# VectorE joins a weight's words in the PSUM bank; other low halves by VectorE; turns moved

## The chip, the cores and the metric

The kernel runs on one core of one Trainium2 chip. The metric is device time in microseconds (us) of one execution, as the median of several runs; less is better. In this program TensorE (PE) multiplies matrices into PSUM, of which eight banks are used; ScalarE (ACT) and VectorE (DVE) work elementwise on PSUM and on SBUF, the main on-chip memory; GpSimd (POOL) works elementwise on SBUF; SyncE (SP) issues the transfers from and to DRAM.

## What is computed

The reference chains three stages over 4 sequences of 768 positions. All arrays are float32; the kernel is handed the three big weights' float64 bits (a low and a high 32-bit word for each number).

```python
for t in range(S):                                   # gated linear attention, 8 heads of 48
    state = alpha[:, :, t, :, None] * state + einsum('bhd,bhe->bhde', k[:, :, t], v[:, :, t])
    y[:, :, t] = einsum('bhd,bhde->bhe', q[:, :, t], state)
x = y as (B, S, 384)
h = maximum(x @ w_in, 0)                             # moe: w_in 384 x 1024
conv_out = three taps of conv_w along S over h       # zero at both ends
x = (h * sigmoid(conv_out)) @ w_out                  # w_out 1024 x 384
xn = layernorm(x) * g_ln                             # moe2
out = x + maximum(xn @ w_ch1, 0) @ w_ch2             # w_ch1 384 x 1536, w_ch2 1536 x 384
```

## The kernel before

The positions are cut into 12 blocks of 256. A block passes through attention (two chunks of 128 positions each, 24 chunks in all), the first feed-forward part (`moe1_*`, 8 slices j of 128 hidden columns), a norm, and the second one (`moe2_a`, 12 slices). Every large product is done in split precision: an operand is a "high" fp32r part and a "low" fp32r rest, and high x high, high x low and low x high are added in PSUM: nine TensorE products for a slice going in (L604 for moe1, L803 for moe2) and six for a slice going out (L690).

**Weights.** w1 (w_in) and w2 (w_out) come in 4 pieces of 2 slices each, w3 (w_ch1) and w4 (w_ch2) in 6. `convert_weight` turns a piece (128 x 768 numbers) into its high and low part. ScalarE copies the scaled high word (L257, to z) and the top byte (L261). VectorE joins both with the rest of the exponent (L264), then puts the sign in (L267): z is now the weight in float32. ScalarE rounds z to the high part (L306). The low part is z minus high, made in one of two ways that the table `LOWS` picks for w1 to w4: "pe" (TensorE multiplies z with an identity matrix and adds minus the high part, L310 and L311, one PSUM bank of 384 columns at a time; ScalarE copies the bank out, L314), or "pool" (one GpSimd subtraction, L317). `LOWS` is pe, pe, pool, pe; the second halves of w3 and w4 follow `LOW2`, pool. An identity product counts as two TensorE entries in the trace.

**Slices.** For moe1, ScalarE clips the slice and makes the first tap (L612, L616), VectorE adds two taps (L620), ScalarE takes the sigmoid (L635), VectorE multiplies (L638), ScalarE copies the high part (L652), and the low part is a VectorE subtraction (L660), or, for the first `BY_PE` blocks, a TensorE product (L354) and a ScalarE copy (L658). Three PSUM banks hold slices ("h"), three hold sums ("acc"), two serve attention and the weights ("att"). An attention chunk costs VectorE two scans (L408, L424) and two maskings (L459), GpSimd two products (L420, L428), and TensorE scores (L450), a transposition (L474), outputs (L518) and a state update (L534).

**Order.** Everything is a step with a turn, a number from the constants at the top (`FIRST`, `LEAD`, `SPACING` and `FETCH` for chunks, `LOADS` and `CONVERT` with their paces for weights, `LAG` from a slice going in to the same slice going out). `Plan.order` places steps one by one on the five engines: of the steps that are ready on an engine, the one with the lowest turn goes first, with costs that it estimates. The result is a fixed order for each engine; on the chip, an engine works its queue strictly in that order and waits on semaphores.

Of the kernel before, what the change touches and what calls it, by code (L numbers as in the profile page):

```python
# [9 lines left out]
F32R = mybir.dt.float32r  # L10
# [11 lines left out]
DM = H * D  # L22
# [22 lines left out]
XN = 1   # L45
X1 = 2 
WAIT = 6
LAG = 5
FIRST = -16, -15, -14, -4, 2
LEAD = 4  # L50
SPACING = 2
FETCH = 12
LOADS = -17, -16, -4, -9.5
LOAD_PACE = 1
CONVERT = -17, -9, 8, 10
CONVERT_PACE = 1.25, 1, 1 
BY_PE = 2, 0
LATER = 0, 8
LOW2 = "pool" 
LOWS = "pe", "pe", "pool", "pe"   # L60


class Plan:
# [137 lines left out]
def act_us(n, scaled=False):  # L201
    return 0.165 + 0.00083 * n + 0.093 * scaled


def dve_us(n, rate=1):
    return 0.15 + 0.00104 * rate * n


def pool_us(n):
    return 0.13 + 0.00215 * n  # L210
# [7 lines left out]
def attn_moe_kernel(ctx: ExitStack, tc, qka, vv, qka_t, v_t, w_in, conv_w, w_out, g_ln, w_ch1, w_ch2, out):  # L218
# [32 lines left out]
    def from_f64(z, raw, n):  # L251

        low, high = raw[:, :n, 0], raw[:, :n, 1]
        zi = z.bitcast(I32)

        def first():
            act.activation(out=z, in_=high.bitcast(F32), func=ACTF.Copy, scale=2.0 ** -112)  # L257

        def top():
            byte = raw[:, :n, :].bitcast(U8)[:, :, 3]  # L260
            act.activation(out=low, in_=byte, func=ACTF.Copy, scale=1 / 32, bias=-15.5 / 32)  # L261

        def join():
            dve.scalar_tensor_tensor(  # L264
                out=zi, in0=zi, scalar=3, in1=low, op0=ALU.logical_shift_left, op1=ALU.bitwise_or
            )
            dve.scalar_tensor_tensor(  # L267
                out=zi, in0=high, scalar=-(2 ** 31), in1=zi, op0=ALU.bitwise_and, op1=ALU.bitwise_or
            )

        yield first
        yield top
        yield join

    raw_w = {}

    def weight_tile(n, j, dtype):
        return const.tile([128, PIECE, 2, DM], dtype, tag=f"w{n}_{j}", name=f"w{n}_{j}", bufs=1)
# [12 lines left out]
    def convert_weight(n, dst, j):  # L291
# [6 lines left out]
            t["f"] = list(from_f64(t["z"], raw.rearrange("p (n w) -> p n w", w=2), m))  # L298
            t["f"][0]()

        def high():
            t["w"] = weight_tile(n, j, F32R)
            for i in range(PIECE):
                dst[j * PIECE + i] = t["w"][:, i]
            t["z"] = t["z"].rearrange("p (j f) -> p j f", j=PIECE)
            act.activation(out=t["w"][:, :, 0], in_=t["z"], func=ACTF.Copy)  # L306

        def low_products(i):
            t[i] = bank("att", "low")[:, :DM]
            pe.matmul(out=t[i], lhsT=ident, rhs=t["z"][:, i], start=True, stop=False)  # L310
            pe.matmul(out=t[i], lhsT=minus, rhs=t["w"][:, i, 0], start=False, stop=True)  # L311

        def low_half(i):
            act.activation(out=t["w"][:, i, 1], in_=t[i], func=ACTF.Copy)  # L314
# [3 lines left out]

        add("act", act_us(m), first, r=[w], new=[z])
        add("act", act_us(m), lambda: t["f"][1](), w=[w])  # L320
        add("dve", 2 * dve_us(m), lambda: t["f"][2](), r=[w], w=[z], port=True)
        add("act", act_us(m), high, r=[z], w=[w])
        low = LOW2 if n > 2 and j >= F2 // 2 // PIECE else LOWS[n - 1]
        if low == "pe":
            for i in range(PIECE):
                b = ring("att", 2)
                add("pe", 0.9, lambda i=i: low_products(i), r=[z, w], new=[b], mode="full")
                add("act", act_us(DM), lambda i=i: low_half(i), r=[b], w=[w])
        elif low == "dve":
            add("dve", dve_us(m), lambda: rest(dve), r=[z], w=[w], port=True)  # L330
        else:
            add("pool", pool_us(m), lambda: rest(pool), r=[z], w=[w], port=True)


    def causal(t):
# [600 lines left out]
    def load_small():  # L936
# [7 lines left out]
        add("sp", dma_us(220), load, new=[("cwr", 0)])  # L944
        add("act", act_us(24), lambda: t["f"][0](), r=[("cwr", 0)], w=[("cw", 0)])
        add("act", act_us(24), lambda: t["f"][1](), w=[("cwr", 0)])
        add("dve", 0.36, lambda: t["f"][2](), r=[("cwr", 0)], w=[("cw", 0)])


    tasks = []  # L950
# [220 lines left out]
```

## Time and profile before

| what | us |
|---|---|
| median of 3 runs (684.97, 686.26, 686.45) | 686.26 |
| the profiled execution, own time | 685.02 |
| its span, first to last instruction | 683.2 |
| first VectorE instruction on a weight (L264) | at 14.15 |
| first moe1 product (L604) | at 53.86 |
| first tap of a moe1 slice on VectorE (L620) | at 57.37 |
| first moe2 product (L803) | at 119.29 |
| last group of products (L690) | at 674.03 |

The profile lists each instruction with start and duration in us from the span's start. An own time is 1.82 us more than its span. TensorE's clock has two levels, 1.2 and 2.4 GHz; the profile gives the mean granted clock of a stretch as a share of the higher one.

### The profile page before, as it was taken

What the parts mean: (1) busy time and instruction counts of PE and PEld (TensorE: products, weight loads), DVE (VectorE), ACT (ScalarE), POOL (GpSimd) and SP (SyncE); (2) the same over time, 40 slices, a digit from 0 to 9 for tenths busy, and PEclk for the clock granted to TensorE, in tenths of its full rate; (3) what the DMA queues carried; (4) which work ended last, traced back from release to release, by engine and by line L of the source; (5) the groups of instructions that cost most, each with busy time, mean ns of one, the idle gap of its engine ahead of it and who ended that gap; (6) DMA issues with size and microseconds to landing.
All of it is one profiled execution on the core that took longest, in us unless ns stands there. A gap on an engine that the chain in (4) does not pass through costs nothing.

```text
span 683.2 us, 14211 instructions
## 1 busy us (share of the span) xinstructions
PE 649.7 (95%) x5788; PEld 612.6 (90%) x5788; DVE 432.5 (63%) x865; ACT 328.6 (48%) x795; POOL 123.9 (18%) x190
## 2 busy tenths in 40 slices
PE   3887999999999999999999999999999999999995
PEld 2546887989999999999999999999999999999994
DVE  5586999898468379448468379358468457365221
ACT  3678799755245236345345346345245335254210
POOL 4052342461121031101021031101021000000000
PEclk9979999999999999999999999999999999999998
DMA  9997201112112012102012012102001000000000
GB/s 316 319 393 229 71 2 48 52 57 64 57 58 76 5 57 81 57 1 80 1 58 79 2 58 80 57 1 81 1 16 39 1 2 24 1 24 1 2 24 27
DMA packets 15736, 44.50 MB, mean 65 GB/s; under 512 B 1472, under 2 KB 4672, under 8 KB 15664
## 3 DMA queue, kind: packets, MB, share of 16 engines
q1 hardware_dynamic: 15664, 43.52, 19.5%
q8 instruction: 47, 0.77, 0.5%
q14 instruction: 25, 0.20, 0.1%
HBM read 38.80 MB, written 4.72 MB: 64 GB/s over the span
## 4 chain that ended last, share of the span: by engine, by line
PE 89%; DVE 4%; ACT 3%; DMA 1%; issue 1%; POOL 0%; SPq 0%; ACTq 0%
PE acc L690 37%; PE h L803 23%; PE h L604 15%; PE y L518 5%; PE s L450 4%; PE u L534 2%; PE low L310 1%; PE h L759 1%; DMA raw<-in_qka 1%; PE kt L474 1%; DVE z L267 1%; DVE z L264 1%; ACT w L261 1%; ACT z L257 0%; ACT w L314 0%
## 5 line engine op out<-in xcount | busy, mean ns | idle before, releaser
L690 PE MATMUL acc<-w,gh 128*128 128x384 f32 x960 | 250.9, 342 | 0.0
L690 PEld LDWEIGHTS acc<-w,gh 128*128 128x128 f32 x960 | 160.9, 188 | 3.4 <-issue 0.8
L690 PE MATMUL acc<-w,gl 128*128 128x384 f32 x480 | 161.3, 336 | 0.0
L816 DVE SCALAR_TENSOR_TENSOR gl<-h,gh 128x256 fp32r<-128x256 f32 x144 | 60.4, 422 | 153.8 <-ACT gh L811 151.9
L811 ACT ACTIVATE gh<-h 128x256 fp32r<-128x256 f32 x144 | 55.3, 384 | 186.5 <-PE acc L690 168.3
L803 PE MATMUL h<-xnh,w 128*128 128x256 f32 x864 | 127.5, 283 | 0.0
L803 PEld LDWEIGHTS h<-xnh,w 128*128 128x128 f32 x864 | 118.4, 188 | 1.0 <-DVE a L424 0.4
L620 DVE SCALAR_TENSOR_TENSOR cv<-h,cw,cv 128x256 f32<-128x256 f32 x192 | 92.2, 481 | 28.5 <-ACT cv L616 24.0
L604 PE MATMUL h<-xh,w 128*128 128x258 f32 x576 | 87.4, 288 | 4.4 <-ACT gl L658 3.3
L690 PEld LDWEIGHTS acc<-w,gl 128*128 128x128 f32 x480 | 90.1, 188 | 0.0
L604 PEld LDWEIGHTS h<-xh,w 128*128 128x128 f32 x576 | 79.5, 191 | 7.7 <-ACT gl L658 4.5
L803 PE MATMUL h<-xnl,w 128*128 128x256 f32 x432 | 74.9, 282 | 0.0
L612 ACT ACTIVATE h<-h 128x258 f32<-128x258 f32 x96 | 35.7, 372 | 61.7 <-PE h L604 59.2
L803 PEld LDWEIGHTS h<-xnl,w 128*128 128x128 f32 x432 | 61.6, 188 | 0.0
L604 PE MATMUL h<-xl,w 128*128 128x258 f32 x288 | 50.4, 283 | 0.0
L635 ACT ACTIVATE cv<-cv 128x256 f32<-128x256 f32 x96 | 39.7, 415 | 21.1 <-DVE cv L620 20.8
L616 ACT ACTIVATE cv<-h,cw 128x256 f32<-128x256 f32 x96 | 45.3, 473 | 1.6
L638 DVE TENSOR_TENSOR h<-h,cv 128x256 f32<-128x256 f32 x96 | 40.6, 424 | 8.2 <-ACT cv L635 5.5
L411 POOL COPY ends<-later 112x4 f32<-112x4 f32 x24 | 5.9, 245 | 217.6 <-DVE later L408 217.6
L428 POOL TENSOR_TENSOR a<-raw,a 112x512 f32<-112x512 f32 x24 | 30.1, 1254 | 69.7 <-DVE a L424 68.4
L604 PEld LDWEIGHTS h<-xl,w 128*128 128x128 f32 x288 | 41.6, 191 | 0.2 <-POOL xl L580 0.2
L652 ACT ACTIVATE gh<-h 128x256 fp32r<-128x256 f32 x96 | 35.8, 380 | 10.2 <-DVE h L638 8.6
(90 smaller groups left out, 778.6 us busy)
## 6 DMA issues: line engine op xcount, KB each, us to landing
raw<-in_qka SPq DMA_DIRECT2D x23, 673.8 KB, 4.7
w<-in_moe_w_ch SPq DMA_DIRECT2D x12, 768.0 KB, 15.3
vraw<-in_vv SPq DMA_DIRECT2D x24, 256.0 KB, 2.7
out<-x SPq DMA_DIRECT2D x11, 384.0 KB, 2.8
w<-in_moe_w_in SPq DMA_DIRECT2D x4, 768.0 KB, 13.3
w<-in_moe_w_out SPq DMA_DIRECT2D x4, 768.0 KB, 14.4
raw<-in_qka SPq DMA_DIRECT2D x1, 448.0 KB, 3.8
out<-x SPq DMA_DIRECT2D x2, 192.0 KB, 3.8
```

Of the source, the lines that this page charges most:

```text
L518: pe.matmul(out=ps[32 * n:32 * n + 32, k * C:(k + 1) * C], lhsT=l, rhs=r, start=m < 4, stop=m >= len(products) - 4, skip_group_check=True,)
L604: pe.matmul(out=ps[:, :T + 2], lhsT=w1[j][:, l, k * 128:(k + 1) * 128], rhs=r[:, k, :], start=n == 0, stop=n == 3 * K1 - 1,)
L612: act.activation(out=t["h"], in_=t["h"], func=ACTF.Relu)
L616: act.activation(out=t["cv"], in_=t["h"][:, 0:T], func=ACTF.Copy, scale=cw[:, 0, j:j + 1])
L620: dve.scalar_tensor_tensor(out=t["cv"], in0=t["h"][:, k:k + T], scalar=cw[:, k, j:j + 1], in1=t["cv"], op0=ALU.mult, op1=ALU.add,)
L635: act.activation(out=t["cv"], in_=t["cv"], func=ACTF.Sigmoid)
L638: dve.tensor_tensor(out=t["h"][:, :T], in0=t["h"][:, 1:T + 1], in1=t["cv"], op=ALU.mult)
L652: act.activation(out=m_t[0, i, j][0], in_=t["h"][:, :T], func=ACTF.Copy)
L690: pe.matmul(out=acc_t[s, i][t][:, :DM], lhsT=l[:, ts], rhs=w[j][:, r], start=j in firsts and n == 0, stop=j + 1 in lasts and n == 2,)
L803: pe.matmul(out=ps[:, :T], lhsT=w3[j][:, l, k * 128:(k + 1) * 128], rhs=r[:, k, :], start=n == 0, stop=n == 3 * K1 - 1,)
L811: act.activation(out=m_t[1, i, j][0], in_=u["ps"][:, :T], func=ACTF.Relu)
L816: dve.scalar_tensor_tensor(out=lo, in0=u["ps"][:, :T], scalar=0.0, in1=hi, op0=ALU.max, op1=ALU.subtract)
```

## The change

Four things change. (1) A "pe" weight gets its low part without the identity: TensorE first writes any product into the bank (`opens`), VectorE writes the joined words with the sign straight into that bank (`sign`, L269 of the new file), ScalarE copies the high part out of the bank, TensorE adds minus the high part to it (`less`), and ScalarE copies the low part out. (2) `LOWS` becomes pe, dve, dve, dve: only w1 goes that way; w2 and the first halves of w3 and w4 get their low part by one VectorE subtraction (L335 of the new file) with both inputs in SBUF. (3) `BY_PE` goes from 2 to 1 block, so block 1's eight low parts move from TensorE and ScalarE to VectorE. (4) The turns move.

```diff
-LAG = 5
-FIRST = -16, -15, -14, -4, 2
+LAG = 4
+FIRST = -12, -15, -14, -6, 2
...
-BY_PE = 2, 0
+BY_PE = 1, 0
...
-LOWS = "pe", "pe", "pool", "pe" 
+LOWS = "pe", "dve", "dve", "dve" 
...
+        def sign(to=z, part=slice(0, n)):
             dve.scalar_tensor_tensor(
-                out=zi, in0=high, scalar=-(2 ** 31), in1=zi, op0=ALU.bitwise_and, op1=ALU.bitwise_or
+                out=to.bitcast(I32), in0=high[:, part], scalar=-(2 ** 31), in1=zi[:, part],
+                op0=ALU.bitwise_and, op1=ALU.bitwise_or,
             )
...
+        banks = [ring("att", 2) for _ in range(PIECE)] if low == "pe" else []
+
+        def opens(i):
+
             t[i] = bank("att", "low")[:, :DM]
-            pe.matmul(out=t[i], lhsT=ident, rhs=t["z"][:, i], start=True, stop=False)
-            pe.matmul(out=t[i], lhsT=minus, rhs=t["w"][:, i, 0], start=False, stop=True)
+            pe.matmul(
+                out=t[i].rearrange("p (k c) -> p k c", k=K1), lhsT=minus,
+                rhs=minus.rearrange("p (o c) -> p o c", o=1).to_broadcast([128, K1, 128]), start=True, stop=True,
+            )
+
+        def sign(i):
+
+            t["f"][3](t[i], slice(i * DM, (i + 1) * DM))
+
+        def high(i=None):
+            if "w" not in t:
+                t["w"] = weight_tile(n, j, F32R)
+                for m in range(PIECE):
+                    dst[j * PIECE + m] = t["w"][:, m]
+            if i is None:
+                t["z"] = t["z"].rearrange("p (j f) -> p j f", j=PIECE)
+                act.activation(out=t["w"][:, :, 0], in_=t["z"], func=ACTF.Copy)
+            else:
+                act.activation(out=t["w"][:, i, 0], in_=t[i], func=ACTF.Copy)
...
+        if not banks:
+            add("dve", 2 * dve_us(m), lambda: (t["f"][2](), t["f"][3]()), r=[w], w=[z], port=True)
+            add("act", act_us(m), high, r=[z], w=[w])
+            engine, us = (dve, dve_us(m)) if low == "dve" else (pool, pool_us(m))
+            add(low, us, lambda: rest(engine), r=[z], w=[w], port=True)
+            return
+        add("dve", dve_us(m), lambda: t["f"][2](), r=[w], w=[z], port=True)
+        for i, b in enumerate(banks):
+            add("pe", 0.000458 * DM, lambda i=i: opens(i), new=[b], mode="full")
+            add("dve", dve_us(DM), lambda i=i: sign(i), r=[w, z], w=[b])
+        for i, b in enumerate(banks):
+            add("act", act_us(DM), lambda i=i: high(i), r=[b], w=[w])
+            add("pe", 0.000458 * DM, lambda i=i: less(t[i], t["w"][:, i, 0]), r=[w], w=[b], mode="full")
+            add("act", act_us(DM), lambda i=i: low_half(i), r=[b], w=[w])
```

The other constants: `LEAD` 4 to 8, `SPACING` 2 to 3, `FETCH` 12 to 10, `LOADS` third value -4 to -8, `CONVERT` from -17, -9, 8, 10 to -19, -9, 9, 11, its paces from 1.25, 1, 1 to 1.25, 1.25, 1.5, `LATER` from 0, 8 to 2, 8. In the new file a line below the changed functions stands 20 lines further down.

What the constants decide is the order of each queue. The first place is VectorE's queue from its first weight piece on. In the rows, z is the joined weight, w1_0 the raw piece 0 of w1, low a PSUM bank, s the scores and pm the masked ones, u and y the update and the outputs of attention. Before:

```order
L264 SCALAR_TENSOR_TENSOR z_158<-z_158,w1_0_109 128x768
L267 SCALAR_TENSOR_TENSOR z_158<-w1_0_109,z_158 128x768
L543 COPY state_80<-u_187 48x4x48 x2
L571 TENSOR_TENSOR xl_203<-y_165,xh_198 128x3x128
L264 SCALAR_TENSOR_TENSOR z_196<-z_196,w2_0_111 128x768
L267 SCALAR_TENSOR_TENSOR z_196<-w2_0_111,z_196 128x768
L459 TENSOR_TENSOR pm_232<-s_210,mask_63 128x512
L459 TENSOR_TENSOR pm_232<-s_211,mask_63 128x512
```

Now:

```order
L264 SCALAR_TENSOR_TENSOR z_144<-z_144,w1_0_113 128x768
L269 SCALAR_TENSOR_TENSOR low_100<-w1_0_113,z_144 128x384
L269 SCALAR_TENSOR_TENSOR low_109<-w1_0_113,z_144 128x384
L479 TENSOR_TENSOR pm_173<-s_150,mask_63 128x512
L264 SCALAR_TENSOR_TENSOR z_163<-z_163,w2_0_115 128x768
L269 SCALAR_TENSOR_TENSOR z_163<-w2_0_115,z_163 128x768
L479 TENSOR_TENSOR pm_173<-s_151,mask_63 128x512
L264 SCALAR_TENSOR_TENSOR z_182<-z_182,w1_1_117 128x768
L269 SCALAR_TENSOR_TENSOR low_186<-w1_1_117,z_182 128x384
L335 TENSOR_TENSOR w2_0_212<-z_163,w2_0_212 128x2x384
L563 COPY state_80<-u_216 48x4x48 x2
```

The sign of a w1 piece is written in two halves into PSUM banks, a w2 piece gets a third VectorE instruction (L335), and chunk 0's maskings now come behind the first weight piece. From VectorE's first weight instruction to the last one ahead of the first tap the queue held 37 instructions and holds 53.

The second place is TensorE's queue around the first moe1 product (h from xh and xl, the two parts of block 0). Before:

```order
L310 MATMUL low_484<-z_374,ident_61 128x384
L311 MATMUL low_484<-w1_3_414,minus_62 128x384
L604 MATMUL h_495<-xh_198,w1_0_206 128x258 x6
L604 MATMUL h_495<-xl_203,w1_0_206 128x258 x3
L604 MATMUL h_508<-xh_198,w1_0_206 128x258 x6
L604 MATMUL h_508<-xl_203,w1_0_206 128x258 x3
L604 MATMUL h_520<-xh_198,w1_1_302 128x258 x6
L604 MATMUL h_520<-xl_203,w1_1_302 128x258 x3
L310 MATMUL low_536<-z_456,ident_61 128x384
L311 MATMUL low_536<-w2_3_518,minus_62 128x384
```

Now:

```order
L470 MATMUL s_493<-a_462,later_393 128x128
L624 MATMUL h_503<-xh_227,w1_0_175 128x258 x6
L624 MATMUL h_503<-xl_240,w1_0_175 128x258 x3
L624 MATMUL h_520<-xh_227,w1_0_175 128x258 x6
L624 MATMUL h_520<-xl_240,w1_0_175 128x258 x3
L494 MATMUL kt_535<-ident_61,later_393 128x112 x4
L624 MATMUL h_541<-xh_227,w1_1_242 128x258 x6
L624 MATMUL h_541<-xl_240,w1_1_242 128x258 x3
L538 MATMUL y_560<-a_462,state_80 32x128 x12
L538 MATMUL y_560<-pm_516,vraw_351 32x128 x16
```

No identity products stand here any more, and the scores of chunk 3, which followed behind the first three slices, now stand ahead of them.

The third place is VectorE's queue at the end of the two moe1 blocks, up to the second xnl, the low part of the normed block 0, which the first moe2 slice needs. Before:

```order
L264 SCALAR_TENSOR_TENSOR z_1122<-z_1122,w3_3_469 128x768
L267 SCALAR_TENSOR_TENSOR z_1122<-w3_3_469,z_1122 128x768
L638 TENSOR_TENSOR h_1103<-h_1103,cv_1141 128x256
L620 SCALAR_TENSOR_TENSOR cv_1199<-h_1143,cw_64,cv_1199 128x256 x2
L778 TENSOR_TENSOR xnl_1209<-h_1179,xnh_1201 128x3x128
L638 TENSOR_TENSOR h_1143<-h_1143,cv_1199 128x256
L459 TENSOR_TENSOR pm_1229<-s_1211,mask_63 128x512
L459 TENSOR_TENSOR pm_1229<-s_1212,mask_63 128x512
L408 SCALAR_TENSOR_TENSOR later_1276<-raw_1192,from_one_78 112x516
L778 TENSOR_TENSOR xnl_1209<-h_1225,xnh_1201 128x3x128
```

Now:

```order
L269 SCALAR_TENSOR_TENSOR z_945<-w3_3_391,z_945 128x768
L658 TENSOR_TENSOR h_1075<-h_1075,cv_1101 128x256
L640 SCALAR_TENSOR_TENSOR cv_1151<-h_1110,cw_64,cv_1151 128x256 x2
L680 TENSOR_TENSOR gl_1167<-h_1075,gh_1164 128x256
L798 TENSOR_TENSOR xnl_1170<-h_1123,xnh_1139 128x3x128
L658 TENSOR_TENSOR h_1110<-h_1110,cv_1151 128x256
L479 TENSOR_TENSOR pm_1184<-s_1141,mask_63 128x512
L680 TENSOR_TENSOR gl_1190<-h_1110,gh_1186 128x256
L798 TENSOR_TENSOR xnl_1170<-h_1172,xnh_1139 128x3x128
```

The subtractions of block 1 (L680) are new on this queue, and a scan of attention (L408) has left it. From the first tap to this second xnl the queue held 92 instructions and holds 95.

## Rows read from the trace of the kernel before

**Rows 1.** The page: busy us and share of the span by engine.
```profile
PE 649.7 (95%) x5788; PEld 612.6 (90%) x5788; DVE 432.5 (63%) x865; ACT 328.6 (48%) x795; POOL 123.9 (18%) x190
```
**Rows 2.** Busy time by stretch, with granted clock, DMA share and GB/s last.
```profile
14.15:57.37 43.22, 35.81 (x299) 23.81 (x300) 30.81 (x38) 30.78 (x55) 13.18 (x16) 0.88 1.03 352
57.37:119.29 61.92, 55.56 (x519) 48.85 (x517) 54.57 (x93) 54.80 (x125) 20.18 (x24) 0.97 0.21 65
80.00:100.00 20.00, 18.79 (x179) 16.80 (x178) 19.28 (x33) 16.84 (x42) 8.35 (x12) 1.00 0.09 31
119.29:674.20 554.91, 554.22 (x4951) 537.14 (x4951) 338.80 (x725) 238.83 (x611) 84.02 (x128) 1.00 0.12 37
674.20:683.20 9.00, 0.51 (x3) 0.19 (x2) 1.08 (x2) 0.00 (x0) 0.00 (x0) 0.66 0.15 50
```
**Rows 3.** VectorE's waits, 12 to 57.4 us: on whom, total, times, longest.
```profile
DVE z L264 <- ACT w L261: 7.2, 3, 4.7
DVE cv L620 <- ACT cv L616: 2.8, 1, 2.8
DVE state L545 <- PE u L534: 1.4, 1, 1.4
```
**Rows 4.** VectorE's waits, 57.4 to 119.29 us.
```profile
DVE h L638 <- ACT cv L635: 3.3, 2, 1.9
DVE pm L459 <- PE s L450: 1.0, 1, 1.0
```
**Rows 5.** TensorE's instructions in order of time: start, us, line, operation.
```profile
53.86 0.99 PE L604 MATMUL h<-xh,w 128*128 128x258 f32 x6 [1.06 <-POOL xh L580]
...
85.40 0.28 PE L354 MATMUL h<-gh,minus 128*128 128x256 f32 x1
85.52 0.89 PE L604 MATMUL h<-xh,w 128*128 128x258 f32 x6
...
86.61 0.81 PE L310 MATMUL low<-z,ident 128*128 128x384 f32 x2
...
87.43 0.89 PE L604 MATMUL h<-xh,w 128*128 128x258 f32 x6
...
119.29 0.88 PE L803 MATMUL h<-xnh,w 128*128 128x256 f32 x6
...
674.03 0.51 PE L690 MATMUL acc<-w,gh 128*128 128x384 f32 x2
```
**Rows 6.** The chain that ended last: one chunk's outputs on TensorE.
```profile
116.54 1.67 PE y L518 x56
```
**Rows 7.** VectorE's instructions in order of time, and GpSimd's beside the slow one.
```profile
14.15 1.57 DVE L264 SCALAR_TENSOR_TENSOR z<-z,w 128x768 int32<-128x768 int32 x1
...
33.05 0.96 DVE L267 SCALAR_TENSOR_TENSOR z<-w,z 128x768 int32<-128x768 int32 x1
33.93 1.23 DVE L408 TENSOR_TENSOR_SCAN later<-raw,from_one 112x516 f32<-112x516 f32 x1
...
36.01 1.17 POOL L420 TENSOR_TENSOR later<-raw,later 112x512 f32<-112x512 f32 x1
36.04 1.96 DVE L267 SCALAR_TENSOR_TENSOR z<-w,z 128x768 int32<-128x768 int32 x1
...
47.57 0.68 DVE L459 TENSOR_TENSOR pm<-s,mask 128x512 f32<-128x512 f32 x1
...
48.38 1.29 DVE L424 TENSOR_TENSOR_SCAN a<-raw,from_end 112x516 f32<-112x516 f32 x1
```
**Rows 8.** Groups of instructions: count, busy us, mean ns, idle before.
```profile
L660 DVE TENSOR_TENSOR gl<-h,gh 128x256 fp32r<-128x256 f32 x80 | 32.7, 418 | 6.8 <-ACT gh L652 4.6 <-PE h L604 0.5
L571 DVE TENSOR_TENSOR xl<-y,xh 128x384 fp32r<-128x384 f32 x24 | 13.1, 546 | 1.9 <-ACT xh L565 1.9
L314 ACT ACTIVATE w<-low 128x384 fp32r<-128x384 f32 x22 | 10.7, 488 | 6.2 <-PE low L311 6.0
L658 ACT ACTIVATE gl<-h 128x256 fp32r<-128x256 f32 x16 | 6.1, 381 | 1.0 <-PE h L354 0.3
```

More of the change, by code (lines that the diff above doesn't have):

```diff
@@ L47 @@
 WAIT = 6
-LAG = 5
-FIRST = -16, -15, -14, -4, 2
[L50 to L53, printed above, removed]
+LAG = 4
+FIRST = -12, -15, -14, -6, 2
+LEAD = 8
+SPACING = 3
+FETCH = 10
+LOADS = -17, -16, -8, -9.5
 LOAD_PACE = 1
-CONVERT = -17, -9, 8, 10
-CONVERT_PACE = 1.25, 1, 1
-BY_PE = 2, 0
-LATER = 0, 8
+CONVERT = -19, -9, 9, 11
+CONVERT_PACE = 1.25, 1.25, 1.5
+BY_PE = 1, 0
+LATER = 2, 8
 LOW2 = "pool"
-LOWS = "pe", "pe", "pool", "pe"
+LOWS = "pe", "dve", "dve", "dve"
 class Plan:
@@ L273, in from_f64 @@
         yield join
+        yield sign
     raw_w = {}
@@ L299, in first @@
             t["f"][0]()
[L301 to L308, printed above, removed]
-            t[i] = bank("att", "low")[:, :DM]
-            pe.matmul(out=t[i], lhsT=ident, rhs=t["z"][:, i], start=True, stop=False)
-            pe.matmul(out=t[i], lhsT=minus, rhs=t["w"][:, i, 0], start=False, stop=True)
+        low = LOW2 if n > 2 and j >= F2 // 2 // PIECE else LOWS[n - 1]
+        banks = [ring("att", 2) for _ in range(PIECE)] if low == "pe" else []
+        def opens(i):
+            t[i] = bank("att", "low")[:, :DM]
+            pe.matmul(
[14 more added lines that the diff above has]
+                act.activation(out=t["w"][:, i, 0], in_=t[i], func=ACTF.Copy)
         def low_half(i):
@@ L320, in convert_weight @@
         add("act", act_us(m), lambda: t["f"][1](), w=[w])
[L321 to L332, printed above, removed]
+        if not banks:
[12 more added lines that the diff above has]
+            add("act", act_us(DM), lambda i=i: low_half(i), r=[b], w=[w])
     def causal(t):
@@ L946, in load_small @@
         add("act", act_us(24), lambda: t["f"][1](), w=[("cwr", 0)])
-        add("dve", 0.36, lambda: t["f"][2](), r=[("cwr", 0)], w=[("cw", 0)])
+        add("dve", 0.36, lambda: (t["f"][2](), t["f"][3]()), r=[("cwr", 0)], w=[("cw", 0)])
     tasks = []
```

## The prediction

> **What bounds the kernel now.** I read the page's engine shares first: TensorE is busy for 95% of the span [rows 1], which seems to say that the change, which takes products away from it, is a gain. A share over the whole span hides stages, so next I cut the span where the work changes: at VectorE's first weight instruction, its first tap, TensorE's first moe2 product and its last products [rows 2, 5, 7]. From 119.29 us on, TensorE is busy for 554.22 of 554.91 us: that stage is bound by TensorE, and its length is the number of its products. Ahead of it, it isn't. From 57.37 to 119.29 us the three engines have 55.56, 54.57 and 54.80 busy us of 61.92: none is full, each waits for the others in turn, though from 80 to 100 us VectorE is busy for 19.28 of 20 us. From 14.15 to 57.37 us VectorE is busy for 30.81 of 43.22 us; its idle time there waits mostly for ScalarE's byte copies, 7.2 us, and for the first tap, 2.8 us [rows 3]. In the next stretch 3.3 us wait for sigmoids [rows 4].
>
> So the question is not how much TensorE saves, but when VectorE, whose queue gets the new work, comes to the end of the second stretch, the second xnl, for which the first moe2 slice waits. I follow that queue: its order before and now is known, and durations come from the rows.
>
> **TensorE's part.** A pair of identity product and subtraction takes 0.82 us at the full clock (86.61 to 87.43), and a product with 256 columns 0.12 us (85.40 to 85.52) [rows 5]. Removed are 22 pairs, 18.0 us, and eight of the 0.12 us products, 1.0 us. Added are eight openings and eight subtractions of 384 columns; at 1.5 times 0.12 they take 2.9 us. TensorE's net is -16.1 us. Of it 14 pairs and all that is added lie ahead of the first tap, where TensorE waits anyway: they are worth nothing by themselves. Eight pairs and the eight products, 7.6 us, leave the second stretch, where TensorE has about 6 us of idle time already. They count only if VectorE and ScalarE get through faster too.
>
> **Ahead of the first tap (14.15 to 57.37).** The start stays: the same five transfers stand ahead of the first weight piece. VectorE's queue grows from 37 instructions to 53:
> - w1's signs: four passes of 0.96 us go, eight half passes into PSUM come. The trace has no such write. Half a pass would be 0.48 us, and a 384-column instruction that reads PSUM takes 0.546 us [rows 7, 8]. I take 0.55, as it is nearest in shape: +4.4 - 3.8 = +0.6 us.
> - Four subtractions for w2, over 768 columns. From 256 columns in 0.418 us and 384 in 0.546 us [rows 8] the slope gives 0.93 us; a 768-column pass takes 0.96 us undisturbed and 1.96 us beside a GpSimd product [rows 7]. I take 0.95 us: +3.8 us.
> - w3's and w4's first pieces are joined here now: four passes of 0.96 us, +3.8 us. They were in the next stretch.
> - Chunk 0's two maskings come behind the first weight piece and chunk 3's ahead of the first tap: four at 0.68 us, +2.7 us [rows 7].
>
> The sum is +10.9 us. An instruction starts about 0.05 us before the one ahead ends (33.93 against 33.05 + 0.96), so sixteen more take 0.8 us less: +10.1 us. Busy time goes from 30.81 to 40.9 us, and the stretch had 12.41 us of idle time, so it nearly fits. What idle time is left lies between nothing and 12.4 us. The 2.8 us ahead of the first tap go, since VectorE now arrives late there; the waits for TensorE's state updates, 1.4 us [rows 3], stay; the waits for byte copies shrink, because VectorE itself is later. I take 3.5 us. The first tap then comes at 14.15 + 40.9 + 3.5 = 58.5 us, 1.2 us later than before. The scores of chunk 3 ahead of the first product cost nothing: VectorE is the later one there. On SP's queue chunk 2's inputs stand one weight piece of 768 KB later, 2.2 us at 352 GB/s [rows 2]; before, they had landed by 33.93 us, when their scan began without a wait [rows 7], so they land by 36.1 us, and VectorE now has some 22 us of queue ahead of that scan, to about 36 us.
>
> **From the first tap to the first moe2 product.** Two weight pieces fewer are joined, -3.8 us; six subtractions of 0.95 us come, +5.7 us, and block 1's eight of 0.418 us, +3.3 us. Of attention, two scans of 1.23, one of 1.29, a short one and three maskings of 0.68 us have left, -6.0 us [rows 7, 8]. The net is -0.8 us: 53.8 busy us. ScalarE loses eight bank copies of 0.488 us and seven of 0.381 us [rows 8], 6.6 us, and TensorE the 7.6 us above, so VectorE should wait less than its 7.35 us; from nothing to 7.35 I take 4.5 us, as the first sigmoids and the scores [rows 4] are waited for as before. That is 92% busy, between the 88% of the stretch and the 96% of its best 20 us [rows 2]. First moe2 product: 58.5 + 53.8 + 4.5 = 116.8 us, against 119.29.
>
> **From there on.** TensorE's products are the same but one group: chunk 5's outputs, 1.67 us [rows 6], which stood ahead of the first moe2 slice, stand behind two of them now. VectorE's queue stays fuller for some 50 us, with the attention that was put off; I add 1.0 us for it (bounds: nothing, and the 3 us that three more scans and maskings take). `LAG` of 4 costs nothing: with three slice banks, TensorE can't start slice j+3 before slice j's low part is made, and in the new order slice j goes out behind that start. The stage takes 554.91 + 1.67 + 1.0 = 557.6 us, the last products are at 674.4 us, and with the 9.0 us behind them [rows 2] the span is 683.4 us. With 1.82 us around it the profiled time is 685.2, against 685.02 before. The median of the runs shown is 686.26, so 1.24 us above its profile, while two of the four known times lie at 685.0 and two at 686.3 to 686.5; I add 0.3 us and predict 685.5 us: no change that can be seen. What this kernel's measurement can tell from no change is about 0.2%, 1.4 us.
>
> **Rivals.**
> - *VectorE runs nearly full, faster.* Its idle time goes to 1.5 us ahead of the first tap, and the second stretch runs at the 96% of 80 to 100 us: 56.5 + 56.0 = 112.5 us, 4.3 us earlier than in my sum, so 681 us. For it: ScalarE and TensorE lose 14 us there, and two engines with room can serve the third in time. Against it: from 57 to 80 us VectorE was waiting for a chain of single results at the start of block 0, and that chain is as long as before.
> - *TensorE's saving counts in full, faster.* If the second stretch were TensorE's, the 7.6 us would come off: 678 us. The busy times of rows 2 speak against it.
> - *Collisions, slower.* The ten new subtractions on VectorE take both inputs from SBUF. In rows 7 the same kind of instruction took 1.96 instead of 0.96 us when GpSimd had begun a product 0.03 us before it. Each collision costs 1.0 us on a queue with almost no idle time left; GpSimd's products for chunks 2 to 5 lie in this time. With five the first moe2 product comes at 121.8 us and the time is 690.5 us; from two on the kernel is slower than measurement can hide. For it: the sum leaves VectorE with 8 us of idle time in 103. Against it: GpSimd loses its own subtractions for w3 here.
>
> The Trainium skill, page "SBUF — State Buffer", section "Who interferes with whom", says that a VectorE instruction with two SBUF inputs contends with a GpSimd instruction that reads SBUF, and that whichever starts first makes the other wait for its whole length. The 1.96 us row agrees. By that rule the halved sign passes are not spared by writing to PSUM, since their inputs still lie in SBUF, and block 1's eight subtractions, which read a bank, are.
>
> **How the numbers follow.** My sum 34%, VectorE nearly full 30%, TensorE in full 8%, collisions 28%. Around my sum I allow 2.5 us to each side, for the idle times taken, so of its 34% some 6 fall on the faster side, 21 within 0.2% and 7 on the slower one. Faster: 30 + 8 + 6 = 44%; same 21%; slower 28 + 7 = 35%. The range for 8 in 10 leaves out the lower end of TensorE's case and more than five collisions: 678 to 691 us. My sum's own range is 683 to 688 us.
>
> **What would show it.** The profile of the changed kernel should have the first tap at 57 to 60 us, VectorE busy for over 90% from 14.15 us to the first moe2 product, and that product at 115 to 119 us; the half sign passes at 0.5 to 0.6 us; TensorE busy throughout from there, for 556 to 558 us. A first moe2 product ahead of 114 us would say that the idle times were taken too long; one behind 120 us, with passes of about 2 us on VectorE, collisions. The prediction also goes wrong if TensorE waits between 120 and 180 us, where VectorE's queue is fuller than it was.

## The result, and the profile after

| | us |
|---|---|
| the changed kernel, median of 4 runs (676.88, 678.16, 681.83, 682.46) | 680.0 |
| the kernel before, 4 runs beside it, median | 685.62 |
| ratio, 95% interval | 0.9919 [0.9892, 0.9945] |
| the changed kernel again, in a later batch, median of 8 runs (677.07 to 681.39) | 678.63 |
| its ratio to the kernel before in that batch | 0.9929 [0.9902, 0.9957] |

The change makes the kernel some 0.75% faster, about 5 us. The profiled execution is the one of 682.46 us, with a span of 680.7. The engine row of the page, which answers to [rows 1]:

```profile
PE 634.5 (93%) x5730; PEld 606.6 (89%) x5730; DVE 448.1 (66%) x887; ACT 323.5 (48%) x777; POOL 124.5 (18%) x187
```

TensorE is busy for 15.2 us less and VectorE for 15.6 us more. Busy time by stretch, as in [rows 2], cut at the same events: first weight instruction on VectorE, first tap, first moe2 product, last products.

```profile
13.24:60.19 46.95, 31.39 (x313) 23.28 (x313) 39.48 (x54) 32.81 (x60) 14.77 (x16) 0.78 1.03 365
60.19:116.41 56.22, 47.77 (x407) 43.01 (x408) 51.33 (x97) 45.18 (x103) 12.77 (x15) 0.91 0.16 44
116.41:671.30 554.89, 554.02 (x5008) 539.75 (x5008) 350.55 (x731) 242.21 (x612) 89.62 (x134) 1.00 0.12 37
```

The first tap comes 2.8 us later than before, the first moe2 product 2.9 us earlier. From there to the last group of products it is 554.55 us (116.41 to 670.96), against 554.74 [rows 5]: nothing was gained or lost in that stage. The events themselves, on VectorE the half passes and subtractions and what was slow, on TensorE the first products of moe1 and moe2 and the last group:

```profile
13.24 1.56 DVE L264 SCALAR_TENSOR_TENSOR z<-z,w 128x768 int32<-128x768 int32 x1 [3.77 <-ACT w L261]
20.33 0.57 DVE L269 SCALAR_TENSOR_TENSOR low<-w,z 128x384 int32<-128x384 int32 x1
20.80 0.95 DVE L335 TENSOR_TENSOR w<-z,w 128x768 fp32r<-128x768 f32 x1
40.84 1.85 DVE L444 TENSOR_TENSOR_SCAN a<-raw,from_end 112x516 f32<-112x516 f32 x1
42.62 2.14 DVE L428 TENSOR_TENSOR_SCAN later<-raw,from_one 112x516 f32<-112x516 f32 x1
45.65 1.82 DVE L269 SCALAR_TENSOR_TENSOR z<-w,z 128x768 int32<-128x768 int32 x1
55.62 1.47 DVE L269 SCALAR_TENSOR_TENSOR z<-w,z 128x768 int32<-128x768 int32 x1
60.19 1.90 DVE L640 SCALAR_TENSOR_TENSOR cv<-h,cw,cv 128x256 f32<-128x256 f32 x4
73.00 2.21 DVE L444 TENSOR_TENSOR_SCAN a<-raw,from_end 112x516 f32<-112x516 f32 x1
```
```profile
54.42 0.99 PE L624 MATMUL h<-xh,w 128*128 128x258 f32 x6
...
116.41 0.76 PE L823 MATMUL h<-xnh,w 128*128 128x256 f32 x5
...
670.96 0.51 PE L710 MATMUL acc<-w,gh 128*128 128x384 f32 x2
```

VectorE's waits from 12 to 60.2 us, which answer to [rows 3]: byte copies (4.4 instead of 7.2 us, 3.8 of them ahead of the first instruction), then state updates and scores of TensorE.

```profile
DVE z L264 <- ACT w L261: 4.4, 2, 3.8
DVE state L565 <- PE u L554: 2.3, 1, 2.3
DVE pm L479 <- PE s L470: 1.6, 2, 1.4
```

TensorE's waits between first tap and first moe2 product will matter below:

```profile
PE h L374 <- ACT gh L672: 3.6, 3, 1.6
PE h L624 <- ACT gl L678: 2.3, 4, 1.2
PE h L624 <- DVE gl L680: 2.3, 4, 1.0
PE y L538 <- DVE pm L479: 0.8, 1, 0.8
```

The changed kernel run again gave a profiled execution of 677.12 us with a span of 675.4. It is the same program, and its two first stretches are 1.9 and 3.0 us shorter:

```profile
12.99:58.09 45.10, 29.93 (x313) 22.08 (x313) 39.57 (x54) 32.77 (x60) 14.76 (x16) 0.81 1.03 366
58.09:111.28 53.19, 44.77 (x408) 40.39 (x409) 51.03 (x97) 45.12 (x103) 12.76 (x15) 0.97 0.21 60
111.28:666.15 554.87, 554.01 (x5008) 539.75 (x5008) 350.71 (x731) 241.87 (x612) 89.53 (x134) 1.00 0.12 37
```

VectorE and ScalarE have the same busy times in both. TensorE has 4.5 us less for as many products, at a higher granted clock: 0.97 instead of 0.91 in the second stretch. So two executions of one program differ by 5.3 us, and of what the profile shows only TensorE's clock differs, in stretches where TensorE is not the full engine. The experiments are therefore compared by the median of many runs, each as a ratio to the kernel before on the same chip; the changed kernel stands at 0.9924 then, the mean of its two ratios, known to some 0.002, or 1.5 us.

### The profile page after: what moved, and what is told of

It is laid out like the page before. It is cut to its first block, busy times and chain, and to the rows that moved or that the text cites. A ratio compares the mean times of both kernels' runs of the same rounds, so it can differ in the third digit from the quotient of the medians.

```text
span 680.7 us, 13950 instructions
## 1 busy us (share of the span) xinstructions
PE 634.5 (93%) x5730; PEld 606.6 (89%) x5730; DVE 448.1 (66%) x887; ACT 323.5 (48%) x777; POOL 124.5 (18%) x187
## 4 chain that ended last, share of the span: by engine, by line
PE 81%; DVE 9%; issue 4%; POOL 3%; ACT 1%; DMA 0%; POOLq 0%; DVEq 0%
PE acc L710 34%; PE h L823 21%; PE h L624 13%; PE y L538 5%; PE s L470 4%; PE u L554 1%; DVE cv L640 1%; PE kt L494 1%; DVE z L269 1%; PE h L779 1%; POOL a L448 1%; DVE z L264 1%; DVE later L428 1%; DVE a L444 1%; POOL later L440 1%
## 5 line engine op out<-in xcount | busy, mean ns | idle before, releaser
L836 DVE SCALAR_TENSOR_TENSOR gl<-h,gh 128x256 fp32r<-128x256 f32 x144 | 60.2, 420 | 136.2 <-ACT gh L831 135.8
L658 DVE TENSOR_TENSOR h<-h,cv 128x256 f32<-128x256 f32 x96 | 40.9, 426 | 17.0 <-ACT cv L655 16.4
L470 PE MATMUL s<-a,later 48*128 48x128 f32 x384 | 31.1, 304 | 13.8 <-POOL a L448 13.6
L470 PEld LDWEIGHTS s<-a,later 48*128 48x128 f32 x384 | 26.0, 204 | 18.2 <-POOL a L448 14.9
```

The costliest lines, as they stand in the source:

```text
L470: pe.matmul(out=t["ps"][g][:, p * C:(p + 1) * C], lhsT=kt[r, p, :], rhs=qd[r, NP - 1 - p, :], start=True, stop=True,)
L658: dve.tensor_tensor(out=t["h"][:, :T], in0=t["h"][:, 1:T + 1], in1=t["cv"], op=ALU.mult)
L836: dve.scalar_tensor_tensor(out=lo, in0=u["ps"][:, :T], scalar=0.0, in1=hi, op0=ALU.max, op1=ALU.subtract)
```

## Experiments

Times in us that follow a ratio are the difference of ratios times 685.

### Turns and method apart

The kernel before with the new turns, `LOWS` and `BY_PE` as they were:

```diff
-LAG = 5
-FIRST = -16, -15, -14, -4, 2
+LAG = 4
+FIRST = -12, -15, -14, -6, 2
...
 BY_PE = 2, 0
...
 LOWS = "pe", "pe", "pool", "pe"
```

> The kernel before with the new turns alone: its low halves are made in the old ways, by identity products and GpSimd. My theory is that VectorE's queue up to the first moe2 product sets the time, and that the other two engines' relief lets it run nearly full. Without the new methods VectorE has some 42 busy us in the second stretch (51.3 less six subtractions of 0.95 and eight of 0.418), but TensorE has 7.6 us more (47.8 to 55.4) and ScalarE 6.6 us more (45.2 to 51.8): no engine is full and each waits for the others as before, so 60 us for that stretch, the first moe2 product at 118 to 120 us, and 684 to 686 us, a ratio of 0.997 to 1.000. Rival, the turns are the whole gain: first moe2 product at 116.4 us, 680 us, ratio 0.992.

Measured: 683.24 us, 0.9969 [0.9959, 0.9979]: 2.1 us faster than before, 3.1 slower than the changed kernel. That is just below the 684 to 686 us of my theory, and 3 us above the rival's 680. The second stretch has, as the theory said, no engine that is full. But the first moe2 product came at 114.27 us, not at 118 to 120, and the last group of products 557.5 us behind it instead of 554.7:

```profile
51.61:114.27 62.66, 55.64 (x467) 47.23 (x466) 52.32 (x91) 54.96 (x129) 20.53 (x20) 1.00 0.31 95
```

The new code with the turns of before (all constants but `BY_PE` and `LOWS` set back):

> The new code with the new ways to make low halves, and the turns of before. By my theory VectorE gets the subtractions (six of 0.95 us and eight of 0.418 us in the second stretch, 9.0 us) and nothing is taken out of that stretch: 54.6 + 9.0 = 63.6 busy us, more than the 61.92 us that the stretch lasted; with 3 us of idle time it lasts 66.5 us, first moe2 product at about 123 us, 689 us, ratio 1.005. Rival, TensorE's saved products are the gain, wherever they stand: 680 us, ratio 0.992 or less.

Measured: 688.58 us, 1.0054 [1.0035, 1.0073]: 3.7 us slower than before. The time is that of my theory, the place is not. The first moe2 product came at 113.46 us, not 123, and TensorE waited behind it:

```profile
54.63:113.46 58.83, 47.71 (x405) 43.05 (x406) 50.73 (x94) 45.85 (x102) 7.76 (x11) 0.88 0.26 78
113.46:140.00 26.54, 22.81 (x209) 21.07 (x209) 25.14 (x34) 16.93 (x31) 14.27 (x11) 1.00 0.12 32
```

From 113.46 to 140 us TensorE, which should be full by now, is busy for 22.81 of 26.54 us and loses 3.7; for 3.1 of them it waits for VectorE's low parts of moe2 slices (L836). VectorE's load alone does not explain that. It is busy for 25.14 us there, but for 25.32 us in as long a time behind the changed kernel's first moe2 product, where TensorE loses nothing; and of the fourteen new subtractions of the second stretch only one stands there. So what stands ahead of those low parts on VectorE's queue should make the difference; no run tests this. It follows that the turns are not decoration: alone they give 2.1 us, the method alone loses 3.7, and together they give 5.2. It also follows that the first moe2 product marks the same point only in kernels whose queues have the same order.

### Whose work counts

Three edits put work on one engine each and leave the order of all queues as it is, except among the last block's products.

```diff
 def products():
...
+    for _ in range(4 if i < 2 else 0):
+        pe.matmul(out=ps[:, :T + 2], lhsT=w1[j][:, 0, :128], rhs=hi[:, 0, :], start=True, stop=True)
```

> The changed kernel, in which each of the 16 moe1 slices of blocks 0 and 1 begins with four more products of 258 columns that are overwritten: 64 products of 0.12 us, 7.7 us that TensorE does more, nearly all between the first tap and the first moe2 product, so that its busy time there goes from 47.8 to about 55 of 56.2 us. The order of all queues stays. If VectorE alone set the time, nothing would change (ratio to before 0.992). Since the slices go through all engines in turn, my theory gives a third of it, 2 to 3 us (first moe2 product at 118.5 to 119.5 us, 682.5 us, ratio 0.996). Rival, TensorE's saving counts in full: 7.7 us, 687.7 us, ratio 1.003.

```diff
 def rest(engine):
+    if engine is dve:
+        engine.tensor_tensor(out=t["w"][:, :, 1], in0=t["z"], in1=t["w"][:, :, 0], op=ALU.subtract)
     engine.tensor_tensor(out=t["w"][:, :, 1], in0=t["z"], in1=t["w"][:, :, 0], op=ALU.subtract)
```

> The changed kernel, in which each of the ten subtractions that VectorE does for weights is done twice with the same result: 9.5 us more on VectorE's queue, 3.8 of them ahead of the first tap and 5.7 behind it. The order of all queues stays. If VectorE's queue sets the time, nearly all of it shows: of 12.4 idle us in the two stretches some 3 are used up, the first moe2 product comes 6 to 8 us later, 687 us, ratio 1.002. Rival, VectorE's work fits into its idle time: less than 3 us, at most 683 us, ratio 0.996 or less.

```diff
 def relu():
+    if i < 2:
+        act.activation(out=t["h"], in_=t["h"], func=ACTF.Relu)
     act.activation(out=t["h"], in_=t["h"], func=ACTF.Relu)
```

> The changed kernel, in which ScalarE clips each of the 16 moe1 slices of blocks 0 and 1 twice, with the same result: 16 times 0.37 us, 5.9 us more, so that it is busy for 51 instead of 45 us of the second stretch. The order of all queues stays. If VectorE's queue alone sets the time: at most 1.5 us more than the changed kernel, ratio to before 0.991 to 0.995. If each engine's work counts, as it did for TensorE's products (6.2 us for 7.7 us) and VectorE's subtractions (10.2 us for 9.5 us): 4 to 6 us more, 683 to 685 us, ratio 0.997 to 1.000.

| engine that does more | work added | ratio to before | against the changed kernel | share that shows |
|---|---|---|---|---|
| TensorE, 64 products | 7.7 us | 0.9996 [0.9979, 1.0014] | +4.9 us | 64% |
| VectorE, ten subtractions | 9.5 us | 1.0046 [1.0028, 1.0064] | +8.4 us | 88% |
| ScalarE, 16 clips | 5.9 us | 0.9986 [0.9973, 0.9998] | +4.2 us | 71% |

The second stretch of each, TensorE's first:

```profile
61.21:119.53 58.32, 51.02 (x459) 46.65 (x460) 51.57 (x97) 45.36 (x103) 11.86 (x15) 0.97 0.14 39
```
```profile
61.25:121.49 60.24, 47.77 (x408) 43.14 (x408) 56.80 (x103) 45.59 (x103) 11.90 (x15) 0.92 0.14 39
```
```profile
61.44:120.18 58.74, 47.71 (x407) 42.99 (x408) 51.53 (x97) 50.15 (x118) 12.11 (x15) 0.91 0.15 40
```

No engine's work is free, not ScalarE's with 45 busy us of 53 to 56 either, and TensorE's counts for more than the third that I had expected. VectorE's share is the largest, but none of the three ran beside the changed kernel, and each loss is known only to some 1.7 us, about 20 to 27 points of a share: which engine counts most is not shown. Of the added work, 3.8 us of VectorE's and 12 of TensorE's products lie ahead of the first tap.

One stretch is free of what differs ahead of it, from TensorE's last low product of block 0 (a low product makes the low part of a slice) to its first moe2 product. It takes 22.33 and 22.37 us in the two executions of the changed kernel, and 24.01 with 24 more products: 1.7 us for 2.9 us of work, at full clock in all three.

My reading is that a slice goes through TensorE, ScalarE and VectorE in turn, and three slice banks let only three be under way: what one engine takes longer, the others can make up only in part. My theory in its strict form, VectorE's queue alone sets the time, falls; so does the rival that only TensorE's work counts.

### Block 1's low parts

`BY_PE` set back to 2, with all turns as in the changed kernel:

> The changed kernel with BY_PE at 2 as before: block 1's eight low parts are made by a TensorE product and a ScalarE copy again. VectorE has 3.3 us less in the second stretch (51.3 to 48.0), TensorE 1.0 us more and ScalarE 3.0 us more (45.2 to 48.2). If VectorE's queue alone sets the end of the stretch, the first moe2 product comes 2 to 3 us earlier, ratio to before 0.988 to 0.989. If the three engines wait for each other in turn, as the run with more TensorE products suggests, taking work from one and giving as much to the two others is worth nothing or loses 1 us: ratio 0.991 to 0.994.

Measured: 687.43 us, 1.0051 [1.0025, 1.0077], 8.7 us slower than the changed kernel; neither theory had that. But the planner made another order of it: the time that it saw freed on VectorE went to joining later weights earlier, nine passes of L264 between first tap and first moe2 product where the changed kernel has five, and the first moe2 product came at 122.29 us. So the next kernel moves the same work and keeps the order, since the planner counts it as VectorE's still:

```diff
-            if by_pe:
+            if by_pe or (i == 1 and not plan.direct):
+                if not by_pe:
+                    take()
                 act.activation(out=lo, in_=g, func=ACTF.Copy)
```

> The changed kernel with its order of turns, in which block 1's eight low parts are made by a TensorE product and a ScalarE copy as before; unlike the run with BY_PE at 2, the planner still counts them as VectorE's, so that the queues keep their order. VectorE has 3.3 us less in the second stretch, TensorE 1.0 us and ScalarE 3.0 us more. If VectorE's queue alone sets the end of the stretch: 2 to 3 us faster than the changed kernel (678.6 us in the batch before), 676 us, ratio to before 0.986 to 0.989. If each engine's work counts, because a slice passes through all of them and three slice banks hold back the next: 0.7 us more work in the chain, within 1.5 us of the changed kernel, ratio 0.990 to 0.995. If the loss of the BY_PE run was the work and not the order, it comes again: 685 us or more, ratio over 1.000.

Measured: 684.96 us, 0.9979 [0.9964, 0.9994]: 3.8 us slower than the changed kernel, between the two last of the three cases. So of the 8.7 us something under half goes with the work, done where the planner put VectorE's subtractions, and the rest with the order; in places that the planner would choose for it, the work may cost less. The work moved was -3.3 us for VectorE and +4.0 us for the two others, and by the shares above it should have come out even (-3.3 x 0.88 + 1.0 x 0.64 + 3.0 x 0.71 = -0.1).

The loss can be found in the trace. From TensorE's last low product of block 0 to its first moe2 product, first the changed kernel, then this run:

```profile
94.08:116.41 22.33, 19.59 (x131) 17.37 (x132) 21.73 (x47) 18.80 (x45) 6.48 (x7) 1.00 0.11 33
```
```profile
94.07:120.21 26.14, 22.14 (x140) 18.66 (x140) 20.86 (x40) 21.33 (x54) 6.58 (x7) 1.00 0.10 28
```

The stretch is 3.8 us longer, all of the loss. TensorE is busy for 2.5 us more, not for 1.0: most of its eight low products stand alone and take 0.28 to 0.39 us each, not 0.12. And it is idle for 4.0 instead of 2.7 us. VectorE is idle for 5.3 instead of 0.6 us, mostly waiting for ScalarE's sigmoids. TensorE's waits in the whole second stretch, and ScalarE's for the low products in this last part of it:

```profile
PE h L374 <- ACT gh L672: 5.6, 6, 2.6
PE h L624 <- ACT gl L680: 4.7, 8, 1.2
```
```profile
ACT gl L680 <- PE h L374: 2.5, 3, 1.5
```

Against the changed kernel TensorE's waits for ScalarE's high part have grown by 2.0 us, but 1.5 of them in block 0, where both kernels do the same; block 1's own low products wait for 0.5 us. What is new in block 1 is on ScalarE's queue. Its copy of a low part waits there for the product, which stands behind other products on TensorE's queue, and the sigmoids behind the copy come late. TensorE's next slice waits for that copy to free the bank, 2.7 us in all, where it waited 2.3 us for VectorE's subtraction. By VectorE a low part is one instruction, and no queue but VectorE's holds anything more for it.

### LAG

```diff
-LAG = 4
+LAG = 5
```

> The changed kernel with LAG at 5 as before. My prediction took the step to 4 as worth nothing, as three slice banks hold a slice's low part back in either case: within 0.2% of the changed kernel, ratio to before 0.990 to 0.994. Rival, with a lag of 4 the slices going out come sooner and serve as work for TensorE while it would wait: then 5 is slower by 1 us or more for each moe1 block ahead of the TensorE-bound stage, ratio 0.995 or more.

Measured: 685.9 us, 1.002 [0.9995, 1.0045], 6.6 us slower than the changed kernel. The rival's size, in another place. The first moe2 product came at 111.40 us, as early as in the best execution above, and TensorE waited behind it:

```profile
135.88 0.62 PE L823 MATMUL h<-xnh,w 128*128 128x256 f32 x3 [1.12 <-ACT w L327]
138.47 0.62 PE L823 MATMUL h<-xnh,w 128*128 128x256 f32 x3 [1.98 <-POOL w L335]
142.58 0.55 PE L779 MATMUL h<-ident,xn 128*128 128x128 f32 x3 [1.73 <-DVE gl L836]
```

The moe2 slices now stand ahead of the weights that they need: two of these rows wait for a piece of w3, 3.1 us. `LAG` also moves slices in the order of all queues, so one constant cannot be judged with the others kept, which fit the other value.

### GpSimd in place of VectorE

The four subtractions for w2 go to GpSimd, in the same places of the order:

```diff
-            add(low, us, lambda: rest(engine), r=[z], w=[w], port=True)
+            add(low, us, lambda: rest(pool if n == 2 else engine), r=[z], w=[w], port=True)
```

> The changed kernel, in which GpSimd does the four subtractions for w2, in the places that they have in the changed kernel's order. VectorE has 3.8 us less (three ahead of the first tap, one behind it), GpSimd 8.3 us more, at 2.07 us each, where it has 14.8 busy us of 47. If VectorE's queue sets the first tap: 2 to 3 us faster than the changed kernel, ratio to before 0.987 to 0.990. Rival, collisions: GpSimd's products for the attention come later, the scores of chunks 2 and 3 wait for them, and passes of VectorE take 1.5 to 2 us instead of 0.96; then it is as slow as the changed kernel or up to 4 us slower, ratio 0.993 to 0.999.

Measured: 681.85 us, 0.9932 [0.991, 0.9954]: the changed kernel's 0.9924 within the uncertainty of 2 us, so no gain shows from 3.8 us less work for VectorE. The rows of VectorE and TensorE at the subtraction for w2's third piece, which GpSimd does from 42.08 to 43.89 us:

```profile
41.30 3.69 DVE L444 TENSOR_TENSOR_SCAN a<-raw,from_end 112x516 f32<-112x516 f32 x1
44.91 2.14 DVE L428 TENSOR_TENSOR_SCAN later<-raw,from_one 112x516 f32<-112x516 f32 x1
```
```profile
48.99 2.08 PE L470 MATMUL s<-a,later 48*128 48x128 f32 x16 [4.90 <-POOL a L448]
```

The first scan takes 1.29 us undisturbed [rows 7], 1.85 us in the changed kernel and 3.69 here, and chunk 2's scores wait 4.90 instead of 3.80 us for GpSimd. This is the rival of collisions, shown at this one place.

### TensorE's clock

The first try to lift TensorE's clock while it waits:

```diff
 def sign(i):
     t["f"][3](t[i], slice(i * DM, (i + 1) * DM))
+def fill():
+    if n == 1 and j > 0:
+        warm(12)
...
     t["ps"] = [bank(b[0], "s") for b in (b0, b1)]
+    if c == 2:
+        warm(36)
```

> The changed kernel, in which TensorE does 108 more products of 128 columns with an identity, whose result nobody reads: twelve behind each subtraction for w1's pieces 1 to 3 and 36 ahead of chunk 2's scores, where TensorE waits between 31 and 47 us. The order of all queues stays. It should lift the granted clock of 0.50 between 36 and 51 us. If the lower clock of the head is only a sign of TensorE's waiting, nothing changes: 0.5 us to either side of the changed kernel, first tap at 60 us. Rival, the lower clock is itself a cost, since VectorE waits there for scores and state updates that took up to twice as long: scores, transposition, outputs and update of chunk 2 take 3 us less, the first tap comes at 58 us, and the time is 1.5 to 2.5 us less than that of the changed kernel, ratio to before 0.988 to 0.990.

Measured: 692.7 us, 1.0111 [1.0075, 1.0147]. It tells nothing of the clock, since the products were far longer than I took them for. The 48 ahead of chunk 2's scores (twelve of them behind w1's last piece) filled 10.9 us, and the scores came at 61.88 instead of 46.71 us:

```profile
51.07 10.88 PE L960 MATMUL warm<-ident 128*128 128x128 f32 x96
```

The changed kernel again, whose result stands above:

> The changed kernel once more, unchanged, beside the three others of this batch on one chip. Its first four runs lay between 676.9 and 682.5 us, and the experiments are measured against it. Both theories expect a ratio to before of 0.990 to 0.995, about 680 us.

The second try is sized by that row, and stands only in TensorE's waits:

```diff
     t["ps"] = [bank(b[0], "s") for b in (b0, b1)]
+    if c in (0, 2):
+        warm(20 if c == 0 else 7)
```

> The changed kernel, in which TensorE does products with an identity that nobody reads, only where it waits: twenty ahead of chunk 0's scores, for which it waits 9.7 us for GpSimd, and seven ahead of chunk 2's scores, where it waits 3.8 us. The identity products cost 0.24 us each at the full clock and about twice that at half, so they fit into both waits. In all runs so far TensorE does its first scores at half clock (2.08 us) and w1's 384-column products in 0.69 instead of 0.44 us, and only in some does the clock rise between 22 and 33 us; those have the first tap at 58.1 to 60.2 us, the others at 60.0 to 62.5. If TensorE's clock ahead of the first tap is on the path: the first products of the head take 0.44 us and the scores 1.2 us, the first tap comes at 55 to 57 us, and the time is 2 to 4 us less than that of the changed kernel, 675 to 677 us, ratio to before 0.986 to 0.990. If VectorE's queue sets the first tap, whatever TensorE's clock: no change, first tap at 58 to 60 us, ratio 0.992 to 0.994.

Measured: 676.3 us, 0.9897 [0.9871, 0.9922]: the fastest of all, but its interval overlaps that of the changed kernel. The profile (of its slowest run, 680.22 us) bears the mechanism out for one step only:

```profile
4.02 6.86 PE L956 MATMUL warm<-ident 128*128 128x128 f32 x40
14.19 1.16 PE L472 MATMUL s<-a,later 48*128 48x128 f32 x16 [3.31 <-POOL a L448]
16.72 0.69 PE L374 MATMUL low<-w,minus 128*128 128x384 f32 x1 [0.63 <-ACT w L329]
```

The first scores take 1.16 instead of 2.08 us, but 2.5 us after their start a product of 384 columns is at 0.69 us again, and the first tap comes at 59.50 us, not at 55 to 57. Chunk 2's scores are at 2.08 us as before. So whether a TensorE kept at 2.4 GHz through the head is worth 2 us or more stays open.

## Why the prediction was right or wrong

The range held the time and the likeliest case did not: 685.5 us, no change, against 680.0. The measured time lies between two of the rivals, VectorE nearly full (681) and TensorE's saving in full (678). The profiled execution's span is 2.7 us shorter than the 683.4 us of my sum: 1.7 us were lost ahead of the first tap, 2.1 won in the second stretch and 2.7 in TensorE's stage, and 0.4 lost behind it. In the execution of 675.4 us the same parts won 0.4, 5.1 and 2.7 us and lost 0.2. So two steps failed, TensorE's stage and the second stretch. By steps:

- **First tap at 58.5 us: right within what executions differ by**, 60.19 and 58.09 in the two, with parts that erred against each other: the start came 0.9 to 1.2 us earlier, VectorE was busy for 39.5 instead of 40.9 us, and idle for 5.5 to 7.5 instead of 3.5, since it also waited for scores and state updates of a TensorE at half clock. I also misread the overlap of neighbours: the rows that I took 0.05 us from give 0.08, which is 0.5 us less.
- **TensorE from the first moe2 product on, +2.7 us: a step that failed**, as nothing was added: 554.89 us, not 557.6. Chunk 5's outputs do stand there (1.9 us more busy time in their groups), but TensorE waits no more for VectorE's fuller queue than before, 0.9 against 0.7 us in all, and its other products take some 3 us less altogether, a few tenths of a per cent each; the runs don't show why.
- **The second stretch, 58.3 us: the other step that failed.** It took 56.2 and 53.2 us. The busy time was 51.3 and not 53.8, though the edits were priced rightly (half passes 0.57, subtractions 0.95 to 0.97). Two things were mis-sized. I took 9.8 us of joins and attention out of the stretch, at undisturbed durations, with one pass too few and two maskings too many; the groups shrank by 10.8 us (joins 5.7, scans 4.3, maskings and reciprocals 0.8). And I left the overlap of neighbours as it was, where a VectorE that waits less overlaps more: all groups together exceed its busy time by 4.1 us before and by 5.6 us now. That is 1.0 and 1.5 of the 2.5 us. Two of the groups before, and after:

```profile
L267 DVE SCALAR_TENSOR_TENSOR z<-w,z 128x768 int32<-128x768 int32 x7 | 7.6, 1084 | 0.2
L408 DVE TENSOR_TENSOR_SCAN later<-raw,from_one 112x516 f32<-112x516 f32 x4 | 5.6, 1400 | 0.5 <-DMA raw<-in_qka 0.5
```
```profile
L269 DVE SCALAR_TENSOR_TENSOR z<-w,z 128x768 int32<-128x768 int32 x5 | 4.8, 957 | 0.2
L428 DVE TENSOR_TENSOR_SCAN later<-raw,from_one 112x516 f32<-112x516 f32 x2 | 2.4, 1223 | 0.0
```

- **Idle time there, 4.5 us:** 4.9 us in one execution and 2.2 in the other. In the faster one VectorE is busy for 96% of the stretch, which is what the first rival assumed for it. But that rival's 1.5 us of idle time ahead of the first tap were 5.5 to 7.5, so its 681 us, near the median of 680.0, are in part luck.
- **TensorE's 7.6 us of products that leave the second stretch "count only if VectorE and ScalarE get through faster too": doubtful.** The run with 7.7 us more products, most of them in that stretch, lost 4.9 us though the two others had no more to do. What taking them away gave is not measured by itself.
- **`BY_PE`, priced as 3.3 us more for VectorE and 3.7 less for the others: incomplete.** In the changed kernel's order it is worth 3.8 us. I had TensorE's low products at 0.12 us each, and the waits between ScalarE's copies and TensorE at nothing. The trace of before had such waits, 2.8 of these 3.3 us in block 1, and I did not read them:

```profile
PE h L604 <- ACT gl L658: 3.3, 5, 1.2
```

- **`LAG` of 4 costs nothing: not contradicted, and not the point.** Set back, it loses 6.6 us, as the order no longer fits the weights.
- **Collisions, 28%: did not decide.** In the changed kernel four passes and scans behind the first instruction and ahead of the first tap, and one behind it, are longer than 1.4 us, as the rows above show; together they are 3.8 us over the undisturbed durations. The kernel before has eight such, 4.9 us over. None of the five is one of the ten new subtractions. In the second stretch GpSimd's busy time fell from 20.18 [rows 2] to 12.77 us, and with it the mean sign pass from 1084 to 957 ns. The Trainium skill, page "SBUF — State Buffer", section "Who interferes with whom", has the one that starts later wait for the other's whole length. The scan of 2.14 us behind the one of 3.69 agrees: it began 1.06 us ahead of the end of a GpSimd product and took 0.9 us longer than undisturbed. The scan of 3.69 us agrees only if it waited for two GpSimd instructions in a row, one that began with it and the subtraction that began 0.78 us later; the rows don't tell.

What is shown is that more work on any of the three engines costs time, and that the turns are needed for the method to pay. That the five microseconds are the sum of block 1's low parts (3.8 us) and a better fit of the rest is argued from these runs, not shown by one.

## What to carry to other kernels

Where no engine is full and a few buffers pass from engine to engine, price an edit on each of them: here 64 to 88% of a microsecond added to any of the three showed, each known to some 25 points. Work that passes from engine to engine can cost more than its busy times, since an instruction that waits at the head of a queue holds back all that is behind it: here a ScalarE copy held back the sigmoids. Read that from the waits of each engine that the work passes through. And when a planner decides the order, test an edit with the order held fixed, as otherwise the test is of two things.

## What the runs showed of the hardware

TensorE's clock in the head differs from execution to execution of the same queue. From 24 to 36 us, with 97 products of TensorE in each, in the changed kernel run again and in the run with block 1's low parts on TensorE (whose queues are the same up to there):

```profile
24.00:36.00 12.00, 6.99 (x97) 4.73 (x95) 10.60 (x18) 10.52 (x20) 0.86 (x3) 0.87 1.03 344
```
```profile
24.00:36.00 12.00, 9.87 (x97) 7.50 (x96) 9.05 (x17) 8.31 (x16) 1.10 (x3) 1.00 1.03 312
```

The second is the slower one, 9.87 busy us for as many products, though its clock column says 1.00. The rows decide: there the same product of 384 columns takes 0.69 us, in the first execution 0.44:

```profile
26.72 0.44 PE L311 MATMUL low<-minus 128*128 128x384 f32 x1 [1.07 <-ACT w L332]
```
```profile
27.71 0.69 PE L311 MATMUL low<-minus 128*128 128x384 f32 x1
```

The column seems to show full speed ahead of the first change that is on record; there durations are the only witness. All executions of the changed kernel and its variants but the one with products ahead have their first scores at 2.08 us, half speed. The Trainium skill, page "TensorE: Matmul & The Clock Gate", section "Part 1: The HAM clock gate", says that the throttled level is where TensorE starts, and that activity releases it; the rows agree with it. Whether products removed from the head bring its lower clock is not shown. Chunk 2's scores took 1.16 us in the kernel before and 2.08 in the changed one, but 2.08 also with the new turns alone, which remove no product.
